# Attention and two feed-forward layers on one core: scores of the later head pairs with q's two parts stacked over 128 rows, a table of priority offsets, and last stores in halves

## The chip, the core and the metric

The kernel runs on one core of a Trainium2 chip. The metric is the device time of one execution in microseconds (us), as a median of several runs. One execution was also recorded by the profiler; all rows shown here come from it.

## What is computed

```python
# q, k, v: (4 batches, 8 heads, 576 rows, 64); f: (4, 8, 576)
scores = q @ k.T / 8
cum = cumsum(log(clip(f, 1e-4, 1)))
scores = where(causal, -1e9, scores + cum[:, None] - cum[None, :])
x = softmax(scores) @ v                  # heads side by side: (2304, 512)
h = maximum(x @ w_in, 0)                 # w_in (512, 2048)
x = (s * h * h + b) @ w_out              # w_out (2048, 512)
h = x @ w2_in                            # w2_in (512, 1024)
solu = h * softmax(h)
out = layer_norm(solu) * g_ln @ w2_out   # (2304, 512)
```

## The kernel before

**A plan written at build time.** Nothing is ordered at run time. `Plan.add` collects some thousands of steps, each with the engine or engines that may do it, an estimated duration, the buffers it reads and writes, and a priority `pri`. `Plan.run` then plays the engines through with these estimates and fixes for each engine the order in which it will issue. On PE (TensorE) the lowest `pri` among the steps that are ready goes first; on ACT, DVE, POOL and SP it is the lowest sum of ready time and `pri`. Elementwise steps (`copy`, `tt`, `move`) can go to the one of two or three engines that would end them first. All transfers are issued by SP, in the planned order.

**Attention.** The 32 heads are worked in 16 pairs, `p` = 0 to 15. A pair's q and k come as one array of 128 rows and 1216 columns: head 0 on rows 0 to 63, head 1 on rows 64 to 127, q in columns 0 to 639 (the last 64 rows of q stand there as a 128-column block with zeros, at `TQ`), k in columns 640 to 1215 (from `K0`). `scores(p, g)` makes a pair's scores in four groups `g` into two PSUM banks, one for each head: `g` = 0 holds the query blocks 0 and 1, `g` = 1 the 64 tail queries of both heads, `g` = 2 the query block 2 (384 columns) and `g` = 3 the block 3 (512 columns). `unit` then takes the row minimum of the negated score (DVE, L730), the exponential (ACT, L776), transposes the result on PE (L791) and moves it to SBUF (L798, L799). `pv` multiplies with v (L860): its matmuls are 64 columns wide in the array, one head beside the other.

**Two ways to make scores.** Pairs 0 to 3 multiply q and k whole, in 32 bits. Pairs 4 to 15 split them: `split_qk` copies the loaded `raw` tile to a rounded high part `hs` (L583) and subtracts that from it for the low part `ts` (L584), 1216 columns on 128 rows each. `s_mm` then adds three products: high q with high k, high q with low k, low q with high k (L669). In groups 0, 2 and 3 a matmul contracts over the 64 rows of one head, and the matmul of the other head, on the other 64 rows, stands right behind it. Group 1 contracts over all 128 rows. There are four pairs of `hs` and `ts`, so a pair can be prepared as soon as the pair four places ahead has its scores; `prep(p + 4)` stands behind `attention(p)` (L1710). `hs[j]` lies where the whole q and k of pair `j` lay.

**Around it.** The first feed-forward layer is fed to PE between the steps of attention as `job` 0 to 5 (256 tokens each; L1078, L1084 to L1086), at a lower priority than attention. Job 5 has its operand in a tile (`g2`) that exists only after all of attention has been planned. The other tokens follow in `block` (L1289), then the second layer (`pair2` L1533, `tail2` L1639). `store` sends each finished 128 by 512 tile of the output in one transfer (L1648).

Of the kernel before, what the change touches and what calls it, by code (L numbers as in the profile page):

```python
# [37 lines left out]
BP = 300  # L38
# [11 lines left out]
PW = 3  # L50
BW0 = 0
# [8 lines left out]
B3 = 0  # L60
# [4 lines left out]
HOLD = 1500  # L65
URGENT = -50000
# [12 lines left out]
class Plan:  # L79
# [42 lines left out]
    def run(self):  # L122
        free, ready, times, ring, lock = {}, {}, [0.0], 0.0, 0.0
# [160 lines left out]
def pool2(n):  # L284
    return 170 + 2.1 * n
# [10 lines left out]
def kernel(  # L296
# [137 lines left out]

    def dma(out, in_, r, w, size, pri=0, rate=340, after=(), slack=0):
        add("SP", 600, lambda: nc.sync.dma_start(out=out, in_=in_), r, w, pri, bytes=size, rate=rate, after=after, slack=slack)
# [69 lines left out]

    def decay_rows(j, n0, w, to, keys):
        t = raw[j][0:BH, 0:w]
        add("DVE", dve2(w), lambda: nc.vector.tensor_scalar(
            out=t, in0=n_[:, 0:w], scalar1=n_[:, n0:n0 + 1], scalar2=1.0 / scale, op0=ALU.subtract, op1=ALU.mult),  # L510
            [("n", 0), ("n", 1)], [("raw", j, x) for x in range(3)], 3000, lk=True, after=[sm_[1, 1]])
        for o, a, b, c in to:
            dma(o.rearrange("p x n -> (p x) n")[:, a:a + c], t[:, b:b + c], [("raw", j, x) for x in range(3)], [(keys, a)], BH * 4 * c, 3000)
# [86 lines left out]
    def prep(p, part=None):  # L600
        load_qk(p, part)
        if p >= NA:
            if p < 2 * NA:
                j = p % NA

                def tile_():
                    hs[j] = keep.tile([128, QK], F32R, tag=f"qkh{j}", name=f"qkh{j}")

                add("NONE", 0, tile_, (), qk_keys("W", p, None) + qk_keys("H", p, None))
            split_qk(p, part, BP)  # L610
# [5 lines left out]
    def prep_dec(p):  # L616
        j = p % 2
        t, u = decs[j], dects[j]
        after = [sc_[p - 2, 1]] + (list(range(*init_)) if p < NA + 2 else [])
# [26 lines left out]

    def scores(p, g):
# [5 lines left out]
        t, h = ((lambda: whole[j]),) * 2 if one_ else ((lambda: ts[j]), (lambda: hs[j]))  # L653
        rk = [(a, j, x) for a in (("W",) if one_ else ("T", "H")) for x in ((0,) if g == 0 else PARTS)]
        if one_:
# [3 lines left out]
        def products(x, c, kc):  # L659
# [7 lines left out]
            if one_:  # L667
                return (h()[o, q_], h()[o, k_]), (one, dks[g % 2][o, kc])
            return (h()[o, q_], h()[o, k_]), (h()[o, q_], t()[o, k_]), (t()[o, q_], h()[o, k_])  # L669
# [13 lines left out]
        def s_mm(r=None):  # L683
            n = 2 if one_ else 3
            for i in r or range(n):
                for two in blocks:
                    for x, o, c, kc, first in two:
                        a, b = products(x, c, kc)[i]
                        nc.tensor.matmul(o, a, b, start=i == 0 and first, stop=i == n - 1, skip_group_check=True)  # L689

# [6 lines left out]
        add("PE", (5 if one_ else 3) * len(blocks) * mm(n), s_mm, rk, [kx, ky], sn[0], tiled="rows" if g != 1 else None)  # L697
# [6 lines left out]
    def rows(p, a, keys, o, ko, to, names, b):  # L704
# [7 lines left out]
        add("DVE", 2 * dve(9) + 60, inverse, (), keys, b)  # L712
# [5 lines left out]
    def unit(s, p, i, two):  # L718
# [15 lines left out]
        if p >= NA:  # L734
# [149 lines left out]
    def value(src, t, kt, raws, b=BW, after=(), slack=0):  # L884
# [7 lines left out]
        if wide:  # L892


            add("ACT", act_s(512), lambda: nc.scalar.activation(
# [105 lines left out]
    def gate(h, kh, n, r, kr, gh, kgh, gl, kgl, b, plus=None):  # L1001
# [28 lines left out]
        add(ways(square, DVE=dve(n), ACT=2 * act_s(n) + 250, POOL=pool2(n) + pool1(n)), 0, 0, ["sb"], [kr], b)  # L1030
        add({"ACT": (act_s(n), lambda: nc.scalar.activation(out=gh(), in_=r, func=AF.Identity, bias=b_sb)),  # L1031
# [3 lines left out]
        add(ways(rest_, DVE=dve(n), POOL=pool2(n) + pool1(n)), 0, 0, [kgh], [kr, kgl], b)  # L1035
# [89 lines left out]
    def x_raw(t0, fresh):  # L1125

        for z in range(2):
            for p in range(2):
# [12 lines left out]
                kw = [("wraw", p), ("wraw", p, "b")]  # L1141
                for a in range(2):
# [192 lines left out]
    def pair_out(t0, partial, b=BMOE):  # L1335

        n0 = len(P.ops)
        for i in range(6):
# [7 lines left out]
            if partial:  # L1346
                dma_late(pv_, view(x2p_d), keys("x2pd"), [kx], 262144, BX)
                add("DVE", dve(512), lambda o=o, src=src: nc.vector.tensor_tensor(out=o(), in0=src(), in1=o(), op=ALU.add), [ksrc], [kx], b - 2000)
# [194 lines left out]
    def soft2(i, d, kd, sm, ks):  # L1543
# [4 lines left out]
        add("ACT", 1090, lambda: A.activation(out=e(), in_=d(), func=AF.Exp, scale=-1.0, bias=sp(1), accum_out=sp(2)), [kd, "m2"], [ke, ks], B3)  # L1548
        add("DVE", 70, lambda: V.tensor_scalar(out=sp(2), in0=sp(2), scalar1=-1.0, scalar2=-1e-9, op0=ALU.mult, op1=ALU.add), (), [ks], B3)
        add("DVE", 75, lambda: V.reciprocal(out=sp(3), in_=sp(2)), (), [ks], B3)  # L1550
        add("DVE", 1140, lambda: V.scalar_tensor_tensor(
            out=e(), in0=d(), scalar=sp(3), in1=e(), op0=ALU.mult, op1=ALU.mult, accum_out=sp(4)), [kd], [ke, ks], B3, lk=True)
        add("DVE", 70, lambda: V.tensor_scalar_mul(out=sp(5), in0=sp(4), scalar1=-1.0 / DFF2), (), [ks], B3)
        add("ACT", 1145, lambda: A.activation(out=d(), in_=e(), func=AF.Square, bias=sp(5), accum_out=sp(6)), [ke], [kd, ks], B3)
# [3 lines left out]
        add("DVE", 663, lambda: V.tensor_scalar(out=d(), in0=e(), scalar1=sp(5), scalar2=sp(7), op0=ALU.add, op1=ALU.mult),  # L1558
# [20 lines left out]
    def tail2(g, rows_):  # L1579
# [123 lines left out]
    U0, BU = 5, 2000  # L1703
    for p in range(NPAIR):
        if 1 <= p < NPAIR - 2:
            prep_v(p + 2)
        if p + 1 < NA:
# [39 lines left out]
    take([(a, j, x) for a in "HT" for j in range(NA) for x in range(3)] + [k for j in range(NA) for k in bkeys(j)])  # L1747
# [117 lines left out]
```

## Time and profile before

| what | value |
|---|---|
| median of 3 runs (lowest, highest) | 758.08 us (757.65, 758.08) |
| the profiled execution | 758.02 us |
| its span, first to last instruction | 756.2 us |
| PE busy | 747.2 us, 99% |
| DVE, ACT, POOL busy | 571.8, 533.8, 247.4 us |
| granted TensorE clock | 1.00 of full speed over the span |
| moved by DMA | 161.03 MB |

The span starts with the first instruction and ends with the last one, the receipt of the last store; the 1.8 us between span and execution lie outside it. A busy time is the union of the instructions' durations. A matmul's duration reaches from the start of its streaming to its last result, so neighbours overlap: what a matmul costs PE is read from the distance between its start and the next one's.

### The profile page before, as it was taken

Reading aid. Unit: us, or ns where it says so; the run is one execution under the profiler, and the core shown is the slowest. Engines: PE = TensorE matmul, PEld = TensorE weight load, DVE = VectorE, ACT = ScalarE, POOL = GpSimd, SP = SyncE. Lnnn points to the kernel's source line nnn. Section 1 sums busy time; section 2 is a strip of 40 time slices with the busy share of each in tenths; the row PEclk is TensorE's granted clock in tenths of the full one; section 3 lists DMA queues with packets and bytes.
Section 4 is the critical chain, followed back from the end, with each engine's and each line's share of the span. In section 5 each row is a group of like instructions: output and inputs, shape, how many; then the busy total and the mean of one; then the engine's idle time right before and its main releaser. Section 6 shows DMA issues by size and latency. Waiting matters only on the chain.

```text
span 756.2 us, 14881 instructions
## 1 busy us (share of the span) xinstructions
PE 747.2 (99%) x5121; PEld 666.4 (88%) x5121; DVE 571.8 (76%) x1263; ACT 533.8 (71%) x1156; POOL 247.4 (33%) x340
## 2 busy tenths in 40 slices
PE   9999999999999999999999999999999999999998
PEld 6678888888878999999999999999987899999998
DVE  8988887675774967687489667888448899888883
ACT  8989888877767868779587678678707676555461
POOL 1242321241220112014074108064203875545241
PEclk9999999999999999999999999999999999999999
DMA  8897798976843527989269992999968111110001
GB/s 292 299 299 219 268 297 261 299 251 191 252 154 102 189 71 257 314 320 361 104 205 324 377 355 67 347 338 371 376 260 301 29 57 57 56 57 29 29 29 56
DMA packets 88562, 161.03 MB, mean 213 GB/s; under 512 B 9160, under 2 KB 41544, under 8 KB 88488
## 3 DMA queue, kind: packets, MB, share of 16 engines
q1 hardware_dynamic: 88488, 160.10, 61.7%
q8 instruction: 40, 0.66, 0.4%
q14 instruction: 34, 0.28, 0.1%
HBM read 106.90 MB, written 53.17 MB: 212 GB/s over the span
## 4 chain that ended last, share of the span: by engine, by line
PE 83%; DMA 5%; POOL 3%; DVE 3%; ACT 2%; issue 2%; SPq 1%; ACTq 0%; POOLq 0%; DVEq 0%
PE h L1289 17%; PE x2h L1639 9%; PE x2w L1533 7%; PE h L1078 6%; PE S L689 5%; PE PT L791 5%; PE x2w L1085 4%; PE x2w L1086 4%; PE x2w L1084 4%; PE x2h L1084 4%; PE x2h L1086 4%; PE x2h L1085 4%; PE O L860 3%; PE x2w L1639 2%; PE h L1593 1%
## 5 line engine op out<-in xcount | busy, mean ns | idle before, releaser
L776 ACT ACTIVATE e<-e,m 128x256 f32<-128x256 f32 (+4 forms) x144 | 83.3, 581 | 6.3 <-DVE m L730 6.2
L1022 DVE SCALAR_TENSOR_TENSOR g<-r,b_sb,g 128x384 fp32r<-128x384 f32 (+1 forms) x87 | 60.2, 694 | 33.8 <-ACT g L1031 30.1
L1084 PE MATMUL x2h<-g,w 128*128 128x256 f32 x216 | 63.1, 292 | 0.0
L1085 PE MATMUL x2h<-g,w 128*128 128x256 f32 x216 | 61.0, 282 | 0.0
L1086 PE MATMUL x2h<-g,w 128*128 128x256 f32 x216 | 61.0, 282 | 0.0
L791 PE MATMUL PT<-ident,e 128*128 128x128 f32 x384 | 59.2, 281 | 0.9 <-ACT pa L798 0.5
L791 PEld LDWEIGHTS PT<-ident,e 128*128 128x128 f32 x384 | 41.9, 140 | 14.0 <-ACT pb L798 2.3
L1031 ACT ACTIVATE g<-r,b_sb 128x384 fp32r<-128x384 f32 (+1 forms) x83 | 52.0, 630 | 1.6 <-DVE r L1012 0.2
L1015 ACT ACTIVATE r<-r,s_sb 128x384 f32<-128x384 f32 (+1 forms) x79 | 50.3, 637 | 2.6
L1078 PE MATMUL h<-xhl,w 128*128 128x256 f32 x360 | 52.0, 290 | 0.1
L730 DVE CUSTOM_DVE_ANT_0 e<-S,dec 128x128 f32<-128x128 f32 (+2 forms) x72 | 34.0, 507 | 17.0 <-PE S L689 16.5
L1078 PEld LDWEIGHTS h<-xhl,w 128*128 128x128 f32 x360 | 45.6, 191 | 0.5 <-DVE xhl L456 0.2
L1014 ACT ACTIVATE r<-r 128x384 f32<-128x384 f32 (+1 forms) x79 | 42.7, 540 | 1.4
L1084 PEld LDWEIGHTS x2h<-g,w 128*128 128x128 f32 x216 | 41.1, 190 | 0.9
L1085 PEld LDWEIGHTS x2h<-g,w 128*128 128x128 f32 x216 | 41.2, 191 | 0.6
L1086 PEld LDWEIGHTS x2h<-g,w 128*128 128x128 f32 x216 | 41.1, 190 | 0.0
L630 POOL TENSOR_SCALAR_AFFINE_SELECT dec<-dec 128x384 f32<-128x384 f32 (+1 forms) x48 | 25.6, 565 | 47.1 <-DMA dec<-dec_d 39.5
L1533 PE MATMUL x2w<-w,xhl 128*128 128x512 f32 x128 | 40.2, 395 | 0.1
L1004 DVE TENSOR_TENSOR r<-h,xo 128x384 f32<-128x384 f32 x54 | 29.6, 552 | 12.5 <-PE h L1289 11.9
L1298 DVE TENSOR_TENSOR xo<-h,xo 128x384 f32<-128x384 f32 x36 | 20.0, 554 | 25.1 <-PE h L1289 19.3
L1008 ACT ACTIVATE r<-h 128x512 f32<-128x512 f32 (+1 forms) x36 | 19.4, 539 | 26.7 <-PE h L1289 21.3
L1005 ACT ACTIVATE r<-r 128x384 f32<-128x384 f32 x53 | 27.3, 519 | 14.0 <-DVE r L1004 13.8
(410 smaller groups left out, 2401.2 us busy)
## 6 DMA issues: line engine op xcount, KB each, us to landing
wraw<-in_moe_w_in_dram SPq DMA_DIRECT2D x24, 512.0 KB
wraw<-in_moe_w_out_dram SPq DMA_DIRECT2D x24, 512.0 KB
raw<-in_qk_dram SPq DMA_DIRECT2D x12, 608.0 KB
dec<-dec_d SPq DMA_DIRECT2D x12, 512.0 KB
b_d<-w SPq DMA_DIRECT2D x12, 512.0 KB
w<-b_d SPq DMA_DIRECT2D x24, 256.0 KB
vs<-in_v_dram SPq DMA_DIRECT2D x16, 320.0 KB
u_d<-wr SPq DMA_DIRECT2D x20, 256.0 KB
```

Source lines behind the costliest of these rows:

```text
L776: nc.scalar.activation(out=e[:, c], in_=e[:, c], func=AF.Exp, scale=-1.0, bias=m[:, j:j + 1], accum_out=rt[:, cols[j]:cols[j] + 1])
L791: nc.tensor.transpose(pt[:, kb, :], e[:, 128 * kb:128 * kb + 128], ident)
L1015: nc.scalar.activation(out=r, in_=r, func=AF.Copy, scale=s_sb)
L1022: nc.vector.scalar_tensor_tensor(out=gl(), in0=r, scalar=b_sb, in1=f32(gh()), op0=ALU.add, op1=ALU.subtract)
L1031: add({"ACT": (act_s(n), lambda: nc.scalar.activation(out=gh(), in_=r, func=AF.Identity, bias=b_sb)), "DVE": (dve2(n), lambda: nc.vector.t ...
L1078: nc.tensor.matmul(t, w_, v_[:, kc, :], start=kc == 0 and first and x == 0, stop=kc == KD - 1 and x == 2, skip_group_check=True)
L1084: nc.tensor.matmul(t, a_, gh, start=start, stop=False, skip_group_check=True)
L1085: nc.tensor.matmul(t, a_, gl, start=False, stop=False, skip_group_check=True)
L1086: nc.tensor.matmul(t, b_, gh, start=False, stop=stop, skip_group_check=True)
L1289: nc.tensor.matmul(o(), s_(x, c), v_()[:, cs], start=start and c == 0 and z == 0, stop=c == 1 and z == 2, skip_group_check=True)
L1533: nc.tensor.matmul(o, s_[:, kc, :], mv[:, c], start=a not in (2, 6) and kc == 0 and z == 0, stop=kc == 1 and z == 2, skip_group_check=True)
L1639: nc.tensor.matmul(bank_[y][0](), p[:, dc], q[:, wc], start=start and c == 0 and z == 0, stop=c == 3 and z == 2, skip_group_check=True)
```

## The change

Pairs 4 to 15 get operands of another layout. For each head, 128 rows hold the high part of its q on rows 0 to 63 and the low part on rows 64 to 127 (columns 0 to 639), and the high part of its k twice, on both halves (columns 640 to 1215). A further tile holds the low part of k, again on both halves. A matmul over 128 rows then adds two products at once, and two of them (with high k, with low k) make the score; the term low times low is added too. `z_mm` does this one head after the other for groups 0, 2 and 3; in group 0 the block 0 takes 128 columns instead of 256. `tail_mm` does group 1 with three matmuls for each bank, the third from a tile to which the low part of k is carried by a transfer inside SBUF. `stack_qk` loads each head's 64 rows twice and makes the parts; there are two sets of four tiles (the four `ts`, the four `hs`), for even and odd pairs, and `prep(p + 2)` stands behind `attention(p)`.

A table `ORDER` adds offsets to the priorities of some hundreds of numbered steps before the plan is played. Several of the plan's estimated durations change. The last pair of output tiles is stored in halves of 256 columns.

```diff
+ORDER = {
+    40: 10904, 77: -15.4, 82: -2239, 91: -2109, 101: 5486, 105: -5120, 108: 304, 110: 546, 113: 9677, 114: 338, 116: 395, 118: 630, 121: -6970, 124:
...
+    14.3, 3526: -1.4, 3533: -251, 3534: -3223, 3539: -8686, 3549: -2.5, 3560: 7.2, 3565: 1117, 3577: 2369, 3586: 5.9, 3596: 263, 3604: 5258, 3609: 8,
+    3611: 6.2, 3614: 3673, 3632: 10.5, 3638: 15, 3645: 9.1, 3646: 9688, 3668: -0.8, 3674: -4192, 3693: 10.7}
...
     def run(self):
+        for n, x in ORDER.items():
+            self.ops[n]["pri"] += x
...
-    return 170 + 2.1 * n
+    return 170 + 2.15 * n + 120 * (n // 512)
...
-    def split_qk(p, part, b):
-        r, kr, c = qk_raw(p, part)
-        t, h, n = ts[p % NA][:, c], (lambda: hs[p % NA][:, c]), c.stop - c.start
-        kt, kh = (qk_keys(a, p, part) for a in ("T", "H"))
-        copy(h, lambda: r, n, kr, kh, b)
-        tt(lambda: t, lambda: r, lambda: f32(h()), n, ALU.subtract, kr + kh, kt, b)
+    def stack(p):
+        return [(lambda i=i: (hs if p % 2 else ts)[i]) for i in range(4)], [("Z", p % 2, i) for i in range(4)]
+
+    def stack_qk(p, b):
+        if p == NA + 1:
...
+            add("NONE", 0, tiles_, (), [k for j in range(NA) for k in qk_keys("W", j, None)] + [("Z", 1, i) + y for i in range(4) for y in ((), (0,), (1,))])
+        a_, ka = stack(p)
+        l, kl, n_, kn = a_[2], ka[2], a_[3], ka[3]
+        for x in range(2):
+            t, kr, h, kq, kk = raw[x], [("raw", x, a) for a in range(2)], a_[x], ka[x], ka[x] + (0,)
+            o = slice(64 * x, 64 * x + 64)
+            for a in range(2):
+                dma(t[64 * a:64 * a + 64], qk[p][64 * x:64 * x + 64], (), [kr[a]], 256 * QK, 0, rate=300)
+            copy(lambda h=h: h()[:, K0:QK], lambda t=t: t[:, K0:QK], S, kr, [kk], b)
+            tt(lambda x=x: l()[:, S * x:S * x + S], lambda t=t: t[:, K0:QK], lambda h=h: f32(h()[:, K0:QK]), S, ALU.subtract,
+               kr + [kk], [kl + (x,)], b)
+            copy(lambda h=h: h()[:, 0:K0], lambda t=t: t[:, 0:K0], K0, kr, [kq], b)
+            copy(lambda o=o: n_()[o, S:S + 128], lambda t=t, o=o: t[o, TQ:TQ + 128], 128, kr, [kn + (x,)], b)
+            tt(lambda h=h: h()[64:128, 0:K0], lambda t=t: t[64:128, 0:K0], lambda h=h: f32(h()[64:128, 0:K0]), K0, ALU.subtract, kr, [kq], b)
+            dma(LazyAp(lambda x=x, o=o: f32(n_()[o, 0:S])), LazyAp(lambda x=x, o=o: f32(l()[o, S * x:S * x + S])), [kl + (x,)], [kn + (x,)], 256 * S, 0,
+                rate=300)
...
-            return (h()[o, q_], h()[o, k_]), (h()[o, q_], t()[o, k_]), (t()[o, q_], h()[o, k_])
...
+        def z_mm():
+            z, l = [f() for f in a_[:2]], a_[2]()
+            if g == 0:
+                todo = [(x, st[:, 256 * u:256 * u + 128 * u + 128], Q0 + 128 * u, 128 * u + 128, u == 0) for x, st in enumerate((sx, sy))
+                        for u in range(2)]
+            else:
+                w = 128 * qbs[0] + 128
+                todo = [(x, st[:, 0:w], w - 128 - EB, w, True) for x, st in enumerate((sx, sy))]
+            for x, o, c, n, first in todo:
+                for low in range(2):
+                    k_ = l[:, S * x:S * x + n] if low else z[x][:, K0:K0 + n]
+                    nc.tensor.matmul(o, z[x][:, c:c + 128], k_, start=first and not low, stop=bool(low), skip_group_check=True)
+
+        def tail_mm():
+            z, m = [f() for f in a_[:2]], a_[3]()
+            for y, st in enumerate((sx, sy)):
+                for i in range(3):
+                    q_, k_ = (m[:, S:S + 128], m[:, 288 * y:288 * y + 288]) if i == 2 else (
+                        z[i][:, TQ:TQ + 128], z[i][:, K0 + 288 * y:K0 + 288 * y + 288])
+                    nc.tensor.matmul(st[:, 0:288], q_, k_, start=i == 0, stop=i == 2, skip_group_check=True)
...
         def store(t, i):
-            add("SP", 650, lambda: nc.sync.dma_start(out=out[i * 128:(i + 1) * 128, :], in_=late["xo"][:, t]), [("xo", t, f) for f in range(2)],
-                [("out", i)], 0, bytes=262144)
+            for f in range(2) if g == NPR - 1 else (None,):
+                c = slice(0, 512) if f is None else slice(256 * f, 256 * f + 256)
+                add("SP", 650, lambda c=c: nc.sync.dma_start(out=out[i * 128:(i + 1) * 128, c], in_=late["xo"][:, t, c]),
+                    [("xo", t, y) for y in (range(2) if f is None else (f,))], [("out", i, f)], 0, bytes=512 * (c.stop - c.start))
...
-        if p + NA < NPAIR:
-            prep(p + NA)
+        for a in ({0: (4,), 1: (), 2: (), 3: (5,)}.get(p, (p + 2,))):
+            if a < NPAIR:
+                prep(a)
```

## Rows read from the trace of the kernel before

**Rows 1.** The page, part 1: busy time, share of span, instructions of each engine.

```profile
PE 747.2 (99%) x5121; PEld 666.4 (88%) x5121; DVE 571.8 (76%) x1263; ACT 533.8 (71%) x1156; POOL 247.4 (33%) x340
```

**Rows 2.** Waits of PE: line, releaser, us in total, times, longest.

```profile
PE x2h L550 <- DVE eps L467: 1.0, 1, 1.0
PE S L689 <- DVE m L730: 1.0, 2, 0.6
```

**Rows 3.** The end of the chain that ended last, 735 to 757 us: start, us, piece.

```profile
752.94 0.42 DVE xo L1645
```

**Rows 4.** Busy time by stretch; last columns: PE clock, DMA share, GB/s.

```profile
40.00:240.00 200.00, 198.97 (x1698) 165.78 (x1694) 147.95 (x409) 160.36 (x421) 54.27 (x91) 1.00 0.75 241
240.00:280.00 40.00, 40.00 (x321) 39.49 (x318) 29.37 (x58) 29.56 (x55) 4.58 (x2) 1.00 0.36 117
300.00:320.00 20.00, 20.00 (x115) 18.84 (x114) 13.62 (x26) 14.48 (x27) 1.36 (x2) 1.00 0.97 340
```

**Rows 5.** Line 689 (scores), 56 to 232 us: count, duration in ns, first and last start.

```profile
L689 PE MATMUL S<-qkh x120: 277/383/501, 56.1 to 230.7; 64*128 64x256 f32 x48, 128*128 128x288 f32 x24, 64*128 64x384 f32 x24, 64*128 64x512 f32 x24
```

**Rows 6.** Timeline of PE, 108.9 to 113.3 us: start, length, instruction.

```profile
109.07 0.50 PE L689 MATMUL S<-qkh 64*128 64x512 f32 x2
...
109.96 0.55 PE L791 MATMUL PT<-ident,e 128*128 128x128 f32 x3
110.35 0.27 PE L793 MATMUL PT<-ident,e 128*64 128x128 f32 x1
110.46 0.49 PE L791 MATMUL PT<-ident,e 128*128 128x128 f32 x3
...
112.10 0.28 PE L1086 MATMUL x2h<-g,w 128*128 128x256 f32 x1
112.31 0.50 PE L689 MATMUL S<-qkh 64*128 64x256 f32 x4
...
113.22 0.33 PE L791 MATMUL PT<-ident,e 128*128 128x128 f32 x1
```

**Rows 7.** Timeline of PE, 115.5 to 121.3 us.

```profile
118.18 2.23 PE L860 MATMUL O<-pb,vs 128*64 128x320 f32 x20
120.34 0.44 PE L689 MATMUL S<-qkh 64*128 64x384 f32 x2
...
121.06 0.44 PE L791 MATMUL PT<-ident,e 128*128 128x128 f32 x2
```

**Rows 8.** The chain that ended last: start, us, piece, instructions in it.

```profile
486.01 3.12 PE h L1289 x18
...
621.07 2.88 PE x2h L1639 x24
626.77 6.83 PE x2w L1533 x30
```

**Rows 9.** Groups by form, DVE and ACT, 40 to 240 us: busy us, mean ns.

```profile
L456 DVE TENSOR_TENSOR qk<-raw,qkh 128x1216 fp32r<-128x1216 f32 x10 | 14.5, 1450 | 0.0
L456 DVE TENSOR_TENSOR w<-wr,w 128x512 fp32r<-128x512 f32 x7 | 4.8, 688 | 2.6 <-ACT w L446 1.8 <-POOL w L448 0.7
L446 ACT CAST qkh<-raw 128x1216 fp32r<-128x1216 f32 x8 | 9.6, 1203 | 1.1 <-PE S L689 1.1
L446 ACT CAST w<-wr 128x512 fp32r<-128x512 f32 x5 | 3.1, 619 | 0.9 <-DVE wr L899 0.9
```

**Rows 10.** DMA, 40 to 240 us.

```profile
DMA packets 29642, 48.11 MB, mean 241 GB/s; under 512 B 3431, under 2 KB 16733, under 8 KB 29616
```

**Rows 11.** Busy time by stretch, the last transfer.

```profile
754.20:755.20 1.00, 0.00 (x0) 0.00 (x0) 0.00 (x0) 0.00 (x0) 0.00 (x0) 1.00 0.68 262
```

**Rows 12.** Groups of PE instructions, 231 to 283 us.

```profile
L1084 PE MATMUL x2h<-g,w 128*128 128x256 f32 x54 | 15.4, 286 | 0.0
...
L1078 PE MATMUL h<-xhl,w 128*128 128x256 f32 x72 | 9.5, 286 | 0.0
L1078 PE MATMUL h<-g,w 128*128 128x256 f32 x72 | 9.3, 283 | 0.0
```

More of the change, by code (lines that the diff above doesn't have):

```diff
@@ L50 @@
 PW = 3
+DECP = ()
 BW0 = 0
@@ L600, in prep @@
     def prep(p, part=None):
[L601 to L610, printed above, removed]
+        if p < NA:
+            load_qk(p, part)
+        else:
+            stack_qk(p, BP)
     def prep_tail(p):
@@ L618, in prep_dec @@
         t, u = decs[j], dects[j]
-        after = [sc_[p - 2, 1]] + (list(range(*init_)) if p < NA + 2 else [])
+        after = [sc_[x] for x in [(p - 2, 1)] if x in sc_] + (list(range(*init_)) + rows_ if p < NA + 2 else [])
         kd = [("decA", 0)]
@@ L645, in early_v, with by_dec @@
             rate=290)
+    def by_dec(p, g):
+        return p in DECP and g > 0
     def scores(p, g):
@@ L652, in scores @@
         one_ = p < NA
-        t, h = ((lambda: whole[j]),) * 2 if one_ else ((lambda: ts[j]), (lambda: hs[j]))
-        rk = [(a, j, x) for a in (("W",) if one_ else ("T", "H")) for x in ((0,) if g == 0 else PARTS)]
-        if one_:
+        h = lambda: whole[j]
+        rk = [("W", j, x) for x in ((0,) if g == 0 else PARTS)]
+        if one_ and not by_dec(p, g):
             rk += [("dk", g % 2, o, y) for o in ((0,) if g < 2 or g == 3 else (0, 256)) for y in (0, 2)] + [("selt", p % 2) if g == 1 else "sel"]
@@ L696, in scores @@
         sc_[p, g] = len(P.ops)
-        add("PE", (5 if one_ else 3) * len(blocks) * mm(n), s_mm, rk, [kx, ky], sn[0], tiled="rows" if g != 1 else None)
+        if one_:
+            add("PE", (4 if by_dec(p, g) else 5) * len(blocks) * mm(n), s_mm, rk, [kx, ky], sn[0], tiled="rows" if g != 1 else None)
+        elif g == 1:
+            add("PE", 6 * mm(n), tail_mm, [k + y for k in ka[:2] for y in ((), (0,))] + [ka[3] + (x,) for x in range(2)], [kx, ky], sn[0])
+        else:
+            add("PE", 4 * (mm(n) + (mm(128) if g == 0 else 0)), z_mm, [k + y for k in ka[:2] for y in ((), (0,))] + [ka[2] + (x,) for x in range(2)],
+                [kx, ky], sn[0])
         return (sx, kx), (sy, ky)
@@ L1028, in ways @@
             return {e: (d, lambda e=e: fn(e), True) for e, d in t.items()}
-        add(ways(square, DVE=dve(n), ACT=2 * act_s(n) + 250, POOL=pool2(n) + pool1(n)), 0, 0, ["sb"], [kr], b)
-        add({"ACT": (act_s(n), lambda: nc.scalar.activation(out=gh(), in_=r, func=AF.Identity, bias=b_sb)),
+        add(ways(square, DVE=dve(n) + 70, ACT=2 * act_s(n) + 250, POOL=pool2(n) + pool1(n)), 0, 0, ["sb"], [kr], b)
+        add({"ACT": (act_s(n) + 105, lambda: nc.scalar.activation(out=gh(), in_=r, func=AF.Identity, bias=b_sb)),
              "DVE": (dve2(n), lambda: nc.vector.tensor_scalar_add(out=gh(), in0=r, scalar1=b_sb), True),
@@ L1034, in gate @@
                  out=gh(), in0=r, scalar1=1.0, scalar2=b_sb, op0=ALU.mult, op1=ALU.add))}, 0, 0, [kr, "ext"] if kgh[:2] == ("G", 1) else [kr], [kgh], b)
[L1035 removed]
+        add(ways(rest_, DVE=dve(n) + 66, POOL=pool2(n) + pool1(n)), 0, 0, [kgh], [kr, kgl], b)
     def job(n, c, fps, b=BMOE):
@@ L1141, in x_raw @@
                 kw = [("wraw", p), ("wraw", p, "b")]
+                take(kw)
                 for a in range(2):
@@ L1703 @@
     U0, BU = 5, 2000
+    for p in DECP:
+        prep_dec(p)
     for p in range(NPAIR):
@@ L1706 @@
             prep_v(p + 2)
+        if p in (NA, NA + 1):
+            take([("R", p % 2, u) for u in range(7)])
         if p + 1 < NA:
@@ L1746 @@
     take([("xo", a) + x for a in range(2) for x in ((), (0,), (1,))] + [("U", i) for i in range(2)])
-    take([(a, j, x) for a in "HT" for j in range(NA) for x in range(3)] + [k for j in range(NA) for k in bkeys(j)])
+    take([("Z", a, i) + y for a in range(2) for i in range(4) for y in ((), (0,), (1,))] + [k for j in range(NA) for k in bkeys(j)])
     take(H(("xx", 2)) + H(("xx", 3)) + bkeys(7))
```

34 lines of the change are left out of this document (22 added, 12 removed), and 32 rows, old and new, of the table ORDER.

## The prediction

> **What bounds the kernel now.** The page's first part comes first: PE is busy for 747.2 of the 756.2 us span [rows 1], so 9.0 us are left in which it does nothing. 1.0 of them lies ahead of the first matmul [rows 2] and 3.3 behind the last one: the final addition starts at 752.94 as PE ends [rows 3], and 756.2 is the receipt of the store. Only 4.7 us lie between. The list of PE's waits agrees: the longest sums are about one microsecond each [rows 2]. No wait for another engine can give back much; time has to come out of PE's own instructions. Busy time is not the measure for that, since durations overlap; the distance between starts is. The stretches show how much cover there is for other work: between 40 and 240 us DVE is busy for 148.0, ACT for 160.4, POOL for 54.3 of 200 us, and the DMA engines for 75% [rows 4]. The granted clock is 1.00 in each of these stretches. The split scores, which the change rewrites, stand between 56.1 and 230.7 us [rows 5], about 15 us a pair.
>
> **Score matmuls, before.** The timeline of PE gives a group's price from its first start to the next step's. Group 3: 109.07 to 109.96, 0.89 us. Group 0: 112.31 to 113.22, 0.91 [rows 6]. Group 2: 120.34 to 121.06, 0.72 [rows 7]. Each also costs something at its edges. The 256-column matmul ahead of group 0 starts at 112.10 and the group only at 112.31, 0.21 us, where neighbours in one mode need 0.12 (2.88 us for 24 [rows 8]): 0.09 to enter. Behind group 3 the first three transposes take 0.39 us, where one alone advances 0.11 (110.35 to 110.46 [rows 6]): 0.06 to leave. So 0.89 + 0.91 + 0.72 + 3 x 0.15 = 2.97 us a pair, 35.6 us for twelve.
>
> **Score matmuls, after.** All of them use the full array, whose pace is in the chain: 384 columns 3.12/18 = 0.173 us, 256 columns 0.120, 512 columns 6.83/30 = 0.228 [rows 8]. Group 2 becomes four matmuls of 384 (0.69), group 3 four of 512 (0.91), group 0 four of 256 (0.48) and four of 128. Nothing in the trace is a rounded product of 128 columns. From below, the slope from 256 to 512 columns, 0.42 ns a column, gives 0.066 us. From above, the 32-bit products with v: 20 matmuls in 2.16 us (118.18 to 120.34 [rows 7]) are two passes over 1216 columns on two heads side by side, 1.8 ns a column, so about 0.22 us for 128. I take the nearest row, a transpose: it loads the full array and streams 128 columns in 0.11 us [rows 6]. That makes 0.44, and 2.52 us a pair, 30.3 us. Taken off: 35.6 - 30.3 = 5.3 us. Not all of it stays: in eight of the twelve pairs group 2 stands right behind the v product, whose own column mode has to be left whatever comes next; I leave 0.15 us for each, 1.2 us. **Scores: -4.1 us**, with bounds -6.2 (0.066) and +1.2 (0.22; 48 x 0.11 = 5.3 more). Group 1 keeps six full-array matmuls of 288 columns: nothing.
>
> The Trainium skill speaks against this edit: TensorEngine Tiling (Array Packing), section Theoretical Speedup, gives up to twice the speed to a contraction of 64 rows or less, because two tiles run at once, and the change gives that up. It also says (section Key Properties) that a change of the tiling mode drains the array. The trace agrees with both: the two heads' matmuls of group 3 need 0.89 us for six times 512 columns, which one after the other would need 1.37, and the edges cost what the sum above says. By the first rule alone the columns to stream rise from 4224 to 5120 a pair.
>
> **Preparation.** It takes more elementwise work. A line through the casts of 512 and 1216 columns (619 and 1203 ns) gives 672, 725 and 300 ns for 576, 640 and 128 columns; one through the subtractions (688 and 1450 ns) gives 757 and 827 [rows 9]. A head takes all five, 3.28 us, a pair 6.56, where now one cast and one subtraction take 2.65. That is 3.9 us more a pair, 47 us in all. The cover is the idle time of 40 to 240 us: 52 us on DVE, 40 on ACT, 146 on POOL [rows 4]; with POOL taking none, DVE and ACT would stand at 89%. A pair's rows are loaded twice and part of k is carried once more: 0.92 MB more a pair, 11 MB beside the 48.1 MB that move in these 200 us [rows 10], 296 GB/s in place of 241. The queue has run at 340 GB/s with its engines 97% busy, and from 240 to 280 us it moves only 117 [rows 4], where weights staged for later can go. SP issues five transfers more a pair. The two carries wait for a subtraction, and what stands behind them on SP is held up meanwhile, the weights and the next pair's rows; the plan issues by ready time, so this wait is short while the estimates hold. I cost all this at **0**, with PE's other work as cover; without that cover it is the rival below.
>
> **Offsets and estimates.** They move steps and do no work. What they can win is the 4.7 us in which PE idles inside the span; what they can lose is not bounded by a row, but the plan orders what is ready, so I allow the same 4.7. The new estimates are longer for DVE, ACT and POOL steps and bring the plan nearer to the profile. Most of the idle time sits in the first pairs, where transfers and engines are both full. I take a third, **-1.5 us**.
>
> **Last stores.** The last 256 KB keep the queue busy for 0.68 us [rows 11]. In halves the first is gone before the final addition, and the second needs half as long: **-0.3 us**. The issue and the receipt stay. Bounds: 0 and -0.7.
>
> **Sum.** -4.1 - 1.5 - 0.3 = -5.9. The profiled execution took 758.02 us (1.8 of it outside the span), the median is 758.08, so they can stand for each other: **752.1 us**.
>
> **Rivals.**
> *The narrow matmul is slow.* If 128 columns cost 0.22 us, group 0 costs 1.36 us where it cost 1.06, and the scores lose 1.2 us instead of winning 4.1: 757.4 us. For it: 32-bit products do cost that per column. Against: the rounded ones of 256 and more columns cost a quarter of it.
>
> *The mode changes stay.* If the edges are not paid by the score groups but by whatever stands beside the v products, only the columns count: 896 more a pair at 0.42 ns, 4.5 us for twelve. 758.0 + 4.5 - 1.8 = 760.7 us. This is the skill's rule of two tiles at once, taken alone. Against it: most score groups have full-array steps on both sides [rows 6].
>
> *Preparation comes late: slower.* The change leaves two sets of operands where there were four, so a pair's preparation can only start when the pair two places ahead has its last scores. From there to its own first group it has 110.0 to 112.31 plus one pair of 15, 17 us; the parts one after the other are 6.6 and the carry some 2. It decides once queueing on DVE and ACT exceeds 8 us: then every pair slips. PE falls back on `job` matmuls. After 231 us it still had 306 of them (3 x 54 + 2 x 72 [rows 12]), 36.7 us at 0.12; the 144 of job 5 need attention finished, so 19.4 us can be drawn forward. A slip of 3 us in ten pairs is 30 us and leaves PE idle for 10.6: 762.7 us. For it: DVE and ACT are 74% and 80% busy there. Against: PE's idle time there is 1.0 us [rows 4], and the preparation is spread over three engines.
>
> *More than forecast.* The offsets close all 4.7 us and the narrow matmul runs at 0.066: 758.0 - 6.2 - 4.7 - 0.3 = 746.8 us.
>
> **How the numbers follow.** Forecast 0.62 (own range 749.5 to 755), narrow matmul 0.12, mode changes stay 0.03, late preparation 0.07, more than forecast 0.16. The range takes in the forecast's own, the near half of the case below and most of the narrow-matmul case: 747.5 to 757.2. About 0.2% (1.5 us) is what can be told from no change: below 756.5 is faster, above 759.6 slower. Faster: 0.62 + 0.16 + 0.03 of the narrow case, 0.81. Same: the other 0.09. Slower: 0.07 + 0.03, 0.10.
>
> **What would show it.** In the profile after, no score matmul from pair 4 on has 64 rows; the sum of the distances from score starts to the next step falls from 35.6 to about 30; a 128-column score matmul advances 0.11 us; PE's busy time falls by about 5 us and its waits do not grow; DVE, ACT and POOL together do about 47 us more; some 11 MB more are moved. The prediction is wrong if waits of PE for DVE, ACT or DMA appear at the scores, if the 128-column distance is near 0.22, or if the offsets change PE's order in the later stages enough to show there.

## The result and the profile after

The changed kernel takes 768.40 us (median of 5 runs, 766.05 to 771.35) beside 758.08 for the kernel before: a ratio of 1.0133, with a 95% interval from 1.0106 to 1.0161. The forecast was 752.1 us, with a range of 747.5 to 757.2. The kernel is 10.3 us slower than before and 16.3 us above the forecast, and the sign was wrong. The profiled execution is the longest of the five, 771.35 us, with a span of 769.4 and a mean granted clock of 0.996. The shortest, 766.05 us, has 1.000: the clock is part of the spread between the five, and the 8 us that even the shortest loses are not the clock's.

Part 1 of the page after, and its line of the transfer queue. They answer to [rows 1] and to the 161.03 MB of the table before.

```profile
PE 748.9 (97%) x5028; PEld 675.9 (88%) x5028; DVE 588.3 (76%) x1282; ACT 538.1 (70%) x1171; POOL 282.1 (37%) x407
...
DMA packets 92883, 172.05 MB, mean 224 GB/s; under 512 B 10152, under 2 KB 43048, under 8 KB 92808
```

PE does nothing for 20.5 us of its span, where it was 9.0. The 11.0 MB more are those that were forecast. Which stretch lost the time is told by the windows of after, which answer to [rows 4] (same columns: PE, PEld, DVE, ACT, POOL busy, PE clock, DMA share, GB/s).

```profile
40.00:240.00 200.00, 186.56 (x1484) 162.53 (x1482) 151.11 (x400) 162.60 (x428) 84.12 (x140) 0.98 0.98 282
...
100.00:120.00 20.00, 17.48 (x143) 15.32 (x142) 15.44 (x40) 17.41 (x45) 9.17 (x17) 1.00 1.01 282
...
140.00:160.00 20.00, 17.60 (x145) 15.13 (x146) 13.67 (x37) 14.91 (x39) 7.09 (x12) 1.00 0.93 230
```

In the 200 us of attention PE is busy for 186.6 us where it was for 199.0, and the DMA engines for 98% of the time where it was 75%. They move 282 GB/s at that, while in [rows 4] 97% went with 340: the queue is full, but not fast. PE's longest waits after, over the span, answer to [rows 2]; under them those of POOL and ACT for the rows of q and k, from 40 to 240 us. The columns are total us, times, longest.

```profile
PE PT L887 <- ACT e L872: 8.5, 8, 2.4
PE PT L887 <- ACT pa L894: 1.4, 1, 1.4
PE PT L887 <- ACT qkh L492: 1.2, 1, 1.2
...
POOL qk L494 <- DMA raw<-in_qk_dram: 25.4, 8, 7.9
...
ACT qk L492 <- DMA raw<-in_qk_dram: 10.1, 7, 3.9
POOL qkh L494 <- DMA raw<-in_qk_dram: 8.1, 5, 2.5
...
ACT qkh L492 <- DMA raw<-in_qk_dram: 3.8, 1, 3.8
```

PE waits for exponentials at its transposes, and hardly at the scores. Why they are late is seen in one place, 158 to 174 us: first the chain (start, us, what), then ACT's timeline and, in its last line, PE's.

```profile
158.62 10.44 DMA raw<-in_qk_dram
...
169.16 0.15 ACT qk L492
169.31 0.43 issue
169.74 0.63 ACT pb L894 x2
170.37 0.73 ACT e L872 x2
171.10 0.04 issue
171.14 1.97 PE PT L887 x8
```

```profile
164.99 0.24 ACT L498 COPY rs<-O 9x128 f32<-9x128 f32 x1
169.16 0.67 ACT L492 CAST qk<-raw 128x576 fp32r<-128x576 f32 x1 [3.93 <-DMA raw<-in_qk_dram]
169.74 0.63 ACT L894 COPY pb<-PT 64x128 f32<-64x128 f32 x2
170.27 0.72 ACT L872 ACTIVATE e<-e,m 128x512 f32<-128x512 f32 x1
...
171.14 1.97 PE L887 MATMUL PT<-ident,e 128*128 128x128 f32 x8 [2.41 <-ACT e L872]
```

A load of 64 rows is issued at 158.62 and lands 10.4 us later. ACT stands at the cast of these rows for 3.9 us. They belong to a later pair, but ACT works in the planned order, so the present pair's copies and exponentials stand behind the cast. PE has its transposes next, idles for 2.4 us, and then runs for a while at the lower of its two clock levels, 1.2 in place of 2.4 GHz: the granted clock is 0.54 from 170 to 175 us and 0.78 in the next 5.

```profile
170.00:175.00 5.00, 3.86 (x18) 3.86 (x19) 3.73 (x9) 4.94 (x12) 5.00 (x9) 0.54 0.89 226
175.00:180.00 5.00, 5.00 (x35) 5.00 (x34) 4.37 (x12) 4.19 (x13) 1.87 (x3) 0.78 0.84 305
```

The score matmuls themselves came out nearly as priced. PE's timeline after answers to [rows 6].

```profile
116.08 0.22 PE L770 MATMUL S<-qk 128*128 128x128 f32 x1
116.14 0.28 PE L770 MATMUL S<-qk,qk 128*128 128x128 f32 x1
116.26 0.33 PE L770 MATMUL S<-qk 128*128 128x256 f32 x1
116.42 0.28 PE L770 MATMUL S<-qk,qk 128*128 128x256 f32 x1
116.54 0.23 PE L770 MATMUL S<-qk 128*128 128x128 f32 x1
...
117.01 0.88 PE L1174 MATMUL h<-xhl,w 128*128 128x256 f32 x6
...
130.03 0.40 PE L770 MATMUL S<-qk 128*128 128x512 f32 x1
...
130.95 0.49 PE L887 MATMUL PT<-ident,e 128*128 128x128 f32 x3
```

Group 0 takes 0.93 us from first start to the next step (0.92 forecast), group 3 0.92 (0.91). The two narrow matmuls advance 0.06 and 0.12 us, a mean of 0.09 where 0.11 was taken, but the first of 256 columns behind them advances 0.16 where 0.12 was: the four together need 0.46, as in the sum. Group 2, not shown here, reads 0.80 us behind transposes where 0.69 was forecast; 0.08 of that is made up ahead of it, for the last transpose then advances 0.03 us in place of 0.11.

### The profile page after: what moved, and what is told of

Its sections match the earlier page's. It is cut to its first block, busy times and chain, and to the rows that moved or that the text cites. A ratio compares the mean times of both kernels' runs of the same rounds, so it can differ in the third digit from the quotient of the medians.

```text
span 769.4 us, 14873 instructions
## 1 busy us (share of the span) xinstructions
PE 748.9 (97%) x5028; PEld 675.9 (88%) x5028; DVE 588.3 (76%) x1282; ACT 538.1 (70%) x1171; POOL 282.1 (37%) x407
## 4 chain that ended last, share of the span: by engine, by line
PE 74%; DMA 14%; ACT 4%; DVE 3%; issue 2%; POOL 2%; SPq 1%; ACTq 0%; DVEq 0%; POOLq 0%
PE h L1386 17%; PE x2w L1630 10%; PE x2h L1736 10%; DMA raw<-in_qk_dram 6%; PE x2w L1181 4%; PE x2w L1182 4%; PE x2w L1180 4%; PE h L1174 4%; PE x2h L1181 4%; PE x2h L1182 4%; PE x2h L1180 4%; PE h L1690 2%; PE PT L887 2%; DMA wraw<-in_moe_w_in_dram 2%; PE x2w L1736 2%
## 5 line engine op out<-in xcount | busy, mean ns | idle before, releaser
L1118 DVE SCALAR_TENSOR_TENSOR g<-r,b_sb,g 128x384 fp32r<-128x384 f32 (+1 forms) x89 | 61.9, 697 | 24.2 <-ACT g L1127 18.4
L887 PE MATMUL PT<-ident,e 128*128 128x128 f32 x384 | 59.5, 282 | 12.4 <-ACT e L872 8.5
L887 PEld LDWEIGHTS PT<-ident,e 128*128 128x128 f32 x384 | 43.9, 142 | 22.0 <-ACT e L872 12.8
L1111 ACT ACTIVATE r<-r,s_sb 128x384 f32<-128x384 f32 (+1 forms) x82 | 52.1, 636 | 2.7
L1174 PE MATMUL h<-xhl,w 128*128 128x256 f32 x360 | 53.7, 296 | 0.0
L1174 PEld LDWEIGHTS h<-xhl,w 128*128 128x128 f32 x360 | 47.9, 199 | 0.4 <-POOL xhl L504 0.2
L1127 ACT ACTIVATE g<-r,b_sb 128x384 fp32r<-128x384 f32 (+1 forms) x74 | 46.8, 633 | 1.2
L1110 ACT ACTIVATE r<-r 128x384 f32<-128x384 f32 (+1 forms) x82 | 44.4, 541 | 1.4
L894 ACT COPY pb<-PT 128x512 f32<-128x512 f32 (+2 forms) x68 | 31.3, 493 | 7.3 <-PE PT L887 6.7
L956 PE MATMUL O<-pb,vs 128*64 128x320 f32 (+2 forms) x320 | 36.3, 371 | 0.0
```

What stands on the lines that cost most here:

```text
L887: nc.tensor.transpose(pt[:, kb, :], e[:, 128 * kb:128 * kb + 128], ident)
L1111: nc.scalar.activation(out=r, in_=r, func=AF.Copy, scale=s_sb)
L1118: nc.vector.scalar_tensor_tensor(out=gl(), in0=r, scalar=b_sb, in1=f32(gh()), op0=ALU.add, op1=ALU.subtract)
L1127: add({"ACT": (act_s(n) + 105, lambda: nc.scalar.activation(out=gh(), in_=r, func=AF.Identity, bias=b_sb)), "DVE": (dve2(n), lambda: nc.ve ...
L1174: nc.tensor.matmul(t, w_, v_[:, kc, :], start=kc == 0 and first and x == 0, stop=kc == KD - 1 and x == 2, skip_group_check=True)
```

## The experiments

Each kernel ran beside the kernel before on the same chip, which took 758.1 to 758.5 us there. The first theory was that the preparation costs more than nothing; the rivals were the new score matmuls, the new order of the plan, the added elementwise work, the waits of single transfers, and the transfers' bytes. The cuts of code below show the lines that matter, with ... where others are left out; several of these kernels compute with rows that are old, mixed or summed, and only their time is of use.

**One part alone, planned anew.** scores_only puts full-array score matmuls into the kernel before; double_loads loads each pair's rows twice there, by halves; half_loads takes the second load of each head out of the changed kernel; no_offsets empties its table.

```diff
# scores_only, in scores(); full_mm is z_mm of the change on the tiles of before
...
+        if not one_ and g != 1:
+            add("PE", 4 * (mm(n) + (mm(128) if g == 0 else 0)), full_mm, rk, [kx, ky], sn[0])
...
# double_loads, in load_qk()
+            for i in range(4):
+                a = i % 2
+                dma(t[64 * a:64 * a + 64], qk[p][64 * a:64 * a + 64, c], (), [ks[a]], 256 * QK, 0, rate=300)
...
# half_loads, in stack_qk(); rows 64 to 127 are set to zero once
-            for a in range(2):
-                dma(t[64 * a:64 * a + 64], qk[p][64 * x:64 * x + 64], (), [kr[a]], 256 * QK, 0, rate=300)
+            dma(t[0:64], qk[p][64 * x:64 * x + 64], (), [kr[0]], 256 * QK, 0, rate=300)
...
# no_offsets
-ORDER = {
...
+ORDER = {}
```

> The kernel before with full-array score matmuls for groups 0, 2 and 3 of pairs 4 to 15, taken from its own tiles: two matmuls over all 128 rows for each bank, in the widths of the change. The two heads are summed into each score, so only the time counts. Loads, casts, subtractions and offsets are those of before. Theory of all three below: the matmuls are cheaper by 4 to 5 us, 753 to 755 us. If the edges of the 64-row mode had not cost anything, 760 us or more.

Measured: 771.3 us, ratio 1.0172 [1.0141, 1.0204].

> The kernel before, with q and k of pairs 4 to 15 loaded in halves of 64 rows and every half twice (four transfers of 304 KB for a pair in place of one of 608 KB); nothing else is changed. Theory A (the transfers fill the DMA queue and what waits for them holds up the exponentials): slower, 762 to 770 us, with PE idle for 5 us more. Theory B (the offsets and estimates order the steps badly) and theory C (the added casts and subtractions crowd DVE, ACT and POOL): 757 to 759 us.

Measured: 785.4 us, 1.0362 [1.0325, 1.0399].

> The kernel after with only the first of each head's two loads; rows 64 to 127 of the raw tiles are zeroed once, so the low part of q is lost and the scores are less exact. Same casts, subtractions, carries and offsets. Theory A: PE's idle time falls to about that of before and the time to 753 to 758 us. Theories B and C: it stays at 764 to 771 us.

Measured: 775.9 us, 1.0229 [1.0201, 1.0258].

> The kernel after with an empty table of offsets; new estimates, loads and matmuls stay. Theory B: 752 to 757 us. Theories A and C: as slow as after or slower, 765 to 775 us.

Measured: 785.0 us, 1.034 [1.0309, 1.037].

All four missed, and on the slow side. Only scores_only lies in a range that was named, that of edges which cost nothing, and same_plan_scores below speaks against it. Each edit also makes the plan choose another order on every engine, and that alone could cost more than the edit. Without the offsets the changed kernel loses 17 us more. So the next kernels keep an order fixed.

**One part alone, order kept.** same_plan_scores has the order of before on every engine and the new matmuls; other_plan_old_scores has the order of scores_only and the old matmuls. The other two double the loads (within one step) or each cast and subtraction.

```diff
# same_plan_scores: same step, same estimate, other matmuls
-        add("PE", (5 if one_ else 3) * len(blocks) * mm(n), s_mm, rk, [kx, ky], ...
+        add("PE", (5 if one_ else 3) * len(blocks) * mm(n), s_mm if one_ or g == 1 else full_mm, rk, [kx, ky], ...
# other_plan_old_scores, against scores_only
-            add("PE", 4 * (mm(n) + (mm(128) if g == 0 else 0)), full_mm, rk, [kx, ky], sn[0])
+            add("PE", 4 * (mm(n) + (mm(128) if g == 0 else 0)), s_mm, rk, [kx, ky], sn[0])
# same_plan_loads
+            add("SP", 600, lambda: [nc.sync.dma_start(out=t[64 * a:64 * a + 64], in_=qk[p][64 * a:64 * a + 64, c]) for a in (0, 1, 0, 1)],
...
# same_plan_splits, after the cast and the subtraction
+                P.ops[i]["ways"][e] = (d, lambda fn=fn: (fn(), fn()), lk)
```

> The kernel before, every engine's order of steps kept as it is, with the full-array score matmuls of scores_only in the place of the old ones (heads summed, so only the time counts). Theory D (the matmuls are cheaper as worked out, and what scores_only lost came from the new order of steps): 753 to 755 us. Theory E (the full-array matmuls themselves hold something up, as the scores of one head now end before the other's or weights are loaded in line): 765 us or more, as scores_only.

Measured: 755.2 us, 0.9963 [0.995, 0.9976].

> The order of steps of scores_only on every engine, with the score matmuls of the kernel before: the same work as before, in another order. Theory D: 772 to 778 us, some 4 us above scores_only. Theory E: 757 to 760 us.

Measured: 774.2 us, 1.0208 [1.018, 1.0236].

The matmuls win 2.9 us at either order (758.1 to 755.2, 774.2 to 771.3); the other order loses 16 us by itself. The order of before is fitted to its kernel to within 1.0 us of idle PE between 40 and 240 us, and a new one starts far behind.

> The kernel before in its own order, with the load of q and k of pairs 4 to 15 issued as four transfers of 64 rows, every half twice, within the one step. Theory A (the queue is full and late): 762 us or more. Theory D: within 3 us of before, 757 to 761 us; double_loads then lost by its new order.

Measured: 810.7 us, 1.0691 [1.0652, 1.073]. This run tells little: the second load writes the rows of the first, and SP waited 71.2 us in all for such loads to land, which the changed kernel does not do.

> The kernel before in its own order, with every cast and subtraction of the split done twice within its step: 2.65 us of elementwise work a pair more, 32 us in all. Theory C (elementwise work crowds the engines): 762 us or more. Theory D: within 3 us of before, 757 to 761 us.

Measured: 782.2 us, 1.0322 [1.0295, 1.0349]. 32 us of elementwise work more cost 24 us in a kernel whose DVE, ACT and POOL are busy for 74%, 80% and 27% of that stretch. Idle shares are no cover where a step stands in the way of the next one. The order was made for the shorter steps, so a part of the 24 may be the order's.

**The changed kernel in its own order.** Here a step stays in the plan and issues less.

```diff
# after_one_load: no second load of a head from pair 5 on; the rows of an earlier load stay there
+                if a and p > NA:
+                    P.ops[-1]["ways"]["SP"] = (600, lambda: None, False)
# after_no_loads: no load of q and k from pair 6 on
+                if p >= NA + 2:
+                    P.ops[-1]["ways"]["SP"] = (600, lambda: None, False)
# after_light_splits: casts and subtractions on a quarter of the columns from pair 6 on
+            f_ = 4 if p >= NA + 2 else 1
...
```

after_no_loads_light joins the last two and leaves out the carries from pair 6 on as well.

> The kernel after in its own order on every engine, without the second load of each head from pair 5 on (the low part of q then comes from older rows, so the scores are less exact): 22 transfers of 304 KB fewer. Theory A (the doubled loads are late and what waits for them holds PE up): 757 to 762 us. Theory F (the order of steps was made with estimates that the chip does not keep, whatever the loads): 765 us or more.

Measured: 755.4 us, 0.996 [0.994, 0.9979], a little less than expected.

> The kernel after in its own order, without any load of q and k from pair 6 on (old rows are used): nothing waits for these transfers any more. Theory A: 753 to 758 us, with no wait of ACT or POOL for the loads. Theory F: 762 us or more.

Measured: 757.2 us, 0.9984 [0.9967, 1.0001].

> The kernel after in its own order, with the casts and subtractions of stack_qk from pair 6 on cut to a quarter of their columns (the other columns keep old values). Theory C (their time crowds the engines): 755 to 760 us. Theory A: 764 us or more, since the waits for the loads stay.

Measured: 769.3 us, 1.015 [1.0107, 1.0193].

> Both of the last two together, and without the carries from pair 6 on: the preparation is nearly gone, the order of steps is that of after. Theories A and C together: 750 to 753 us, which is before less what the matmuls save. Theory F: 758 us or more even so.

Measured: 754.4 us, 0.9955 [0.9936, 0.9973], a little more than expected.

22 transfers of 0.3 MB fewer give back 13 us; casts and subtractions on a quarter of the columns give back nothing while the loads stay. So the second loads are the cost, and the order of the changed kernel is good enough without them.

**What about the loads.** The cost can lie in their bytes, their issue, memory rows that are read twice, or their form. after_tiny_second keeps the transfer and drops its bytes; after_other_rows keeps bytes and form and reads other rows; after_joined moves the same bytes in one transfer of 128 rows; shifted loads each head once and makes the second half on the engines, with the full result.

```diff
# after_tiny_second
+                c_ = slice(0, 16) if a and p > NA else slice(0, QK)
# after_other_rows
+                y_ = NPAIR - 1 - p if a and p > NA else p
# after_joined (the second step issues nothing)
...
+                r_ = slice(0, 128) if p > NA else slice(64 * a, 64 * a + 64)
+                dma(t[r_], qk[p][r_ if p > NA else slice(64 * x, 64 * x + 64)], (), [kr[a]], 256 * QK, 0, rate=300)
# shifted: one load of 64 rows; the cast of k and its subtraction write both halves, one after the other,
# and so does the cast of q for the second head
...
+                    dma(t[o], qk[p][o], (), [("raw", x, a)], 256 * QK, 0, rate=300)
...
+                two(copy, [(lambda h=h, y=y: h()[y, ks_], lambda t=t, o=o: t[o, ks_]) for y in R], S, kr, [kk], b)
...
```

> The changed kernel with its own order; from pair 5 on the second load of each head brings 16 of the 1216 columns only, so the low part of q is made from rows left by an earlier load. The issues on SP and all waits stay; 0.3 MB less for each of 22 transfers, as in after_one_load (755.4 us). If the bytes are the cost: 755 to 757. If one more issue and wait on SP is the cost: near 768. If each has a part: about 762.

Measured: 757.8 us, 0.9983 [0.9966, 1.0], 0.8 above what was expected of the bytes and far from 768.

> The changed kernel with its own order; from pair 5 on the second load of each head reads the rows of another pair, so the scores are made from mixed rows. Same bytes, same form, same waits. If the bytes are the cost: 768, as the changed kernel. If it is that one row is read twice in short order: 755 to 758.

Measured: 769.0 us, 1.0129 [1.0105, 1.0153].

> The changed kernel with its own order; from pair 5 on each head's two loads of 64 rows become one load of 128 rows (of both heads, so the halves hold different heads and the scores are made from mixed rows). Same bytes, one transfer less a head. If the bytes fill the queue whatever their form: 766 to 769. If two transfers of 64 rows are what is slow (301 ns a packet against 227 before): 755 to 759, with packets of about 230 ns again.

Measured: 756.3 us, 0.9979 [0.9958, 1.0001].

> The changed kernel with its own order and the same result; from pair 5 on each head's 64 rows are loaded once, and the second half of the operands is made by the engines: the cast of k and its subtraction run twice on 64 rows each, and for the odd head the cast of q too. 22 transfers fewer, about 22 x (0.7 + 0.95) + 11 x 0.7 = 44 us more elementwise work in all. If the load is what costs and the engines have room, as the run with light splits says: 755 to 759. If the engines' queues are full: over 765.

Measured: 776.8 us, 1.0231 [1.0207, 1.0255]. It was expected at 755 to 759 if the engines have room, and they have not: ACT waits for the rows for only 0.9 us, and the added elementwise work costs 21 us against after_one_load, which loads as little and took 755.4.

It is neither the issue nor the memory rows, and not the bytes as such: after_joined moves more in the same stretch and loses nothing. What goes with the time is ACT's wait for the rows of q and k from 40 to 240 us: 13.2 to 18.7 us in the three kernels that took 768 to 769 us (the changed one, after_light_splits, after_other_rows), 0.3 to 1.4 in after_one_load, after_tiny_second and after_joined. POOL waits for rows for 8 to 21 us in these fast ones too, at no visible cost. The window of after_joined, and that of after_other_rows:

```profile
40.00:240.00 200.00, 196.14 (x1602) 172.90 (x1600) 160.44 (x423) 171.63 (x452) 89.71 (x140) 1.00 0.93 294
```

```profile
40.00:240.00 200.00, 189.20 (x1517) 164.44 (x1512) 154.23 (x406) 164.76 (x433) 84.18 (x140) 0.99 0.97 284
```

That is 294 GB/s at 93%, against 284 at 97%. The difference sits in the packets of 4864 bytes, one for each row. The table has them from the transfer records of the traces, between 40 and 240 us:

```
kernel             transfers of q and k          packets   mean ns
before             128 rows                         1025       227
after              64 rows, each row twice          2673       301
after_other_rows   64 rows                          2631       292
after_one_load     64 rows, once                    1341       297
after_joined       128 rows                         2573       225
```

**The form by itself, and the way out.** same_plan_halves sends each load of the kernel before as two transfers of 64 rows. doubled_input gives the changed kernel an array in which each head's 64 rows stand twice, so a head comes in one transfer of 128; the array is laid out so before the kernel starts, outside its time.

```diff
# same_plan_halves, in load_qk()
+            add("SP", 600, lambda: [nc.sync.dma_start(out=t[64 * a:64 * a + 64], in_=qk[p][64 * a:64 * a + 64, c]) for a in (0, 1)],
...
# doubled_input, in stack_qk() (the second step issues nothing) and where the arrays are laid out
-                dma(t[64 * a:64 * a + 64], qk[p][64 * x:64 * x + 64], (), [kr[a]], 256 * QK, 0, rate=300)
+                dma(t, qk2[p - NA][x], (), [kr[a]], 256 * QK, 0, rate=300)
...
+    inputs["qk2"] = _np.repeat(qk.reshape(b * h // 2, 2, 1, d, -1)[4:], 2, axis=2).reshape(b * h // 2 - 4, 2, 2 * d, -1)
```

> The changed kernel with its own order and its full computation; the array of q and k holds each head's 64 rows twice, one copy behind the other, so each head comes in one transfer of 128 rows (24 transfers in place of 48, same bytes). If the form of the transfers is the cost: 755 to 757, packets of 4864 bytes near 225 ns as in after_joined, PE's waits for the rows gone. If after_joined won because something else in it was lighter: over 762.

Measured: 756.7 us, 0.9984 [0.9969, 0.9999]; packets of 4864 bytes 227 ns. ACT waits for the rows in one place only, as its casts show (busy us, mean ns, idle time before them):

```profile
L493 ACT CAST qk<-raw 128x640 fp32r<-128x640 f32 x3 | 2.2, 723 | 0.2 <-DMA raw<-in_qk_dram 0.2
```

> The kernel before with its own order; from pair 4 on each pair's load of 128 rows goes as two transfers of 64 rows each, same bytes, nothing done twice. If the form makes packets slow: 290 to 310 ns in place of 227, 5 us more of queue time in a queue that is 75% busy, so 758 to 760 in all. If packets are slow only because the queue is full: 227 ns again and 758.

Measured: 760.6 us, 1.003 [1.0018, 1.0043], 0.6 above the range; packets 301 ns, the queue 80% busy in place of 75%:

```profile
40.00:240.00 200.00, 196.06 (x1664) 162.53 (x1663) 146.22 (x407) 158.96 (x420) 55.51 (x96) 1.00 0.80 240
```

So the form slows the packet with the queue far from full. The windows of doubled_input follow, the second of a stretch in which PE idled for 2.4 us in the changed kernel:

```profile
40.00:240.00 200.00, 194.50 (x1591) 172.17 (x1591) 160.58 (x423) 172.48 (x453) 92.79 (x141) 1.00 0.93 295
...
140.00:160.00 20.00, 20.00 (x165) 18.31 (x164) 15.47 (x42) 18.58 (x50) 8.73 (x12) 1.00 0.98 329
```

In that stretch the queue is as full as in the changed kernel (98%, and 93% there), but it moves 329 GB/s in place of 230, and PE does not idle at all. The other packets of the stretch are not the same in both kernels, so 329 against 230 is not the price of the form alone; 227 against 301 ns is. This is the one kernel here that computes the whole result and is faster than before, by 0.16%.

## Why the prediction was wrong

**The step that failed** is in Preparation: "A pair's rows are loaded twice ... I cost all this at **0**". The bytes were right, and 296 GB/s was right for transfers of 128 rows (295 in doubled_input). What was wrong is the price of a byte: the text took the queue's best rate, 340 GB/s, as the room it had, without looking at what kind of transfer made it. Loads of 64 rows take 301 ns a packet where 227 were paid before. In the 200 us that is 2673 x (301 - 227) / 16 = 12.4 us of all 16 engines' time, in a queue that stands at 98% with it and at 93% without. Undoing it gives back 11.7 us (768.4 to 756.7): more than the 10.3 that the kernel lost, and 11.7 of the 16.3 between forecast and result. That 12.4 and 11.7 are so near is luck, since queue time is not kernel time: in same_plan_halves 1091 packets at 301 ns make 5.0 us of queue time and cost 2.3 us.

The Trainium skill has the rule that would have told the direction: SBUF — State Buffer, section "Can I just issue two DMAs to hit both halves?", says that a transfer's ports are picked by its own span of partitions, that two transfers are not fused into one, and that only one transfer over all 128 partitions reaches all 16 ports of SBUF. This case's traces agree in sign with 301 and 227 ns; that ports are the mechanism is the page's word, and no run here shows it.

**Late preparation** is the rival that was given 0.07. That preparation comes late and leaves PE without its next step was right, and its 762.7 us are on the right side, 5.7 short. The rest of its chain was not: it named queueing on DVE and ACT, and after_light_splits cuts that work to a quarter of the columns for nothing; what is late are the rows. Nor did it see that a cast which waits holds up the exponentials of the present pair, for ACT does nothing past it. PE's idle time was not to grow, and went from 9.0 to 20.5 us, but at the transposes and not, as the text looked for it, at the scores.

**Elementwise work.** 47 us more were forecast. DVE, ACT and POOL together are busy for 160.6 + 172.5 + 92.8 = 425.9 us between 40 and 240 us in doubled_input and were for 362.6 [rows 4]: 63 more. The casts on ACT came out as interpolated, at 666 to 730 ns. The subtractions were too cheap, on DVE (the first two lines, doubled_input) and above all on POOL, which does one in two pieces (the last, after):

```profile
L503 DVE TENSOR_TENSOR qkh<-raw,qkh 128x576 fp32r<-128x576 f32 x10 | 9.1, 907 | 0.1
L503 DVE TENSOR_TENSOR qkh<-raw,qkh 64x640 fp32r<-64x640 f32 x9 | 8.5, 941 | 1.3 <-POOL qkh L495 1.0
L504 POOL TENSOR_TENSOR qkh<-raw,qkh 64x320 fp32r<-64x320 f32 x6 | 6.1, 1041 | 0.2
```

These are 907 and 941 ns, and two pieces of 1041 ns on POOL, where 757 and 827 were interpolated from rows of ACT and DVE alone. The cover was real here (after_no_loads_light is only 2.8 us faster than after_no_loads), but not wide: shifted and same_plan_splits lose 21 and 24 us with some 44 and 32 us more.

**Scores.** The mechanism held, and the two rivals against it (a slow narrow matmul, mode changes that stay) fell. In same_plan_scores PE advances 0.12 us ahead of a score group behind full-array matmuls, where it was 0.21, and its busy time is 745.0 us against 747.2. Of the 4.1 us, 2.9 arrive. Behind the v products nothing is won: group 2 takes 0.80 us there, where 0.72 and 0.06 to leave were paid.

**Offsets.** -1.5 us was the wrong question. They do not win a little in a fitted order; they bring a new order near to fitting. Without them the changed kernel takes 785.0, with them 768.4. Order, preparation and last stores together, with the form mended, come to 756.7 - 758.3 + 2.9 = +1.3 us where -1.5 and -0.3 stood. PE's busy time falls to 742.4 us in doubled_input, by the 5 us or so that were forecast, but its idle time grows from 9.0 to 12.6, and from 40 to 60 us alone, where pair 4 starts, PE idles for 3.9 us more (before, then doubled_input):

```profile
40.00:60.00 20.00, 19.60 (x159) 15.60 (x154) 16.32 (x42) 16.65 (x41) 6.61 (x13) 1.00 0.89 283
40.00:60.00 20.00, 15.71 (x114) 11.76 (x112) 14.27 (x38) 16.47 (x42) 8.91 (x17) 1.00 0.88 271
```

Whether order or preparation is behind it, the runs don't tell.

**Halves of the last stores.** From the start of the last elementwise instruction to the end of the span it was 3.26 us (752.94 to 756.2), after it is 3.07 (766.33 to 769.4), in doubled_input 3.51 (751.49 to 755.0). The -0.3 can't be told from the spread.

The sum as measured: scores -2.9, order, preparation and stores +1.3, form of the transfers +11.7, together +10.1 us of the 10.3. The 1.3 is what the other two leave over, so the sum closes by itself and proves nothing; the 2.9 and the 11.7 are measured. Against the forecast of -5.9 that is 16.0 us: 11.7 for the form, 1.2 for the scores, 3.1 for the rest.

## What to carry to other kernels

Price added transfers by their form, with the duration of a packet of the same shape, and not by the best rate that the queue has shown: a queue with 25% to spare was filled by transfers of 64 rows that fit when they came as 128. When an edit changes the plan, measure it at a fixed order first; here the order was worth 16 us and the edit 3. An engine's idle share is cover only for work that waits for nothing, since one late operand holds all that is planned behind it on its engine.

## What the runs showed of the hardware that was not expected

A packet of 4864 bytes takes on the mean 225 to 228 ns in transfers of 128 rows (245 in same_plan_splits) and 290 to 333 ns in transfers of 64, over all kernels here, and 301 ns with the queue at 80% as at 98%. Whether it is the number of rows or the half of SBUF that they fall on, no run separates.

A rounded matmul of 128 columns over the full array advances 0.06 us in front of another one and 0.12 in front of one of 256 columns, which then advances 0.16 to 0.17 in place of 0.12.

A cast or subtraction of 64 rows costs no less than one of 128: the cast of 64x576 on ACT took 670 ns in shifted and that of 128x576 took 666 to 670 in doubled_input; the subtractions on DVE took 862 to 886 and 802 to 907.
